# Token tiles normalized on GpSimd, an unmasked pair kept selected behind causal ones, and the gate moved behind the transpose

## The chip, the cores and the metric

The kernel runs on one core of one Trainium2 chip. The metric is the device time of one execution in microseconds, from start to finish, with inputs and outputs in the chip's main memory. Five engines work side by side and each takes its own instructions strictly in order: TensorE (PE, matrix products into the accumulator memory PSUM), VectorE (DVE), ScalarE (ACT), GpSimd (POOL) and SyncE (SP, which here only issues DMA transfers). They wait for one another by semaphores. PSUM has eight banks of 128 x 512 float32.

## The reference

Four residual layers in the order A, B, A, B act on 2048 tokens of width 512 with 32 heads of width 16. Each starts with a layer norm without weights.

```python
def _A_ref(x, wq, wk, wv, wo, beta):      # "infini-attention", 4 segments of 512 tokens
    ...
    for s in range(N):
        logits = einsum('bhqd,bhkd->bhqk', qs, ks) * scale + causal_mask
        a_dot = softmax(logits) @ vs
        a_mem = phi(qs) @ M / (phi(qs) @ z + 1e-6)
        o = g * a_mem + (1.0 - g) * a_dot          # g = sigmoid(beta), one number per head
        M = M + phi(ks)^T @ vs ;  z = z + sum(phi(ks))
    return concat(o) @ wo

def _B_ref(x, wqkv, wo):                   # plain attention, every query against all 2048 keys
    q, k, v = split(x @ wqkv)
    return softmax(q @ k^T * Dh**-0.5) @ v @ wo

x = x + _A_ref(layernorm(x), ...) ; x = x + _B_ref(layernorm(x), ...)    # twice
```

The exponentials dominate: with a head width of 16, a product of queries and keys gives far more elements to exponentiate than it costs to compute.

## The kernel before

The program is written by a Python planner (class `Builder`), which appends instructions to one list per engine. It keeps an estimated end time for every engine and uses these estimates, credits and limits (the class constants) to decide what to append next. The order of each engine's list is therefore fixed when the program is built, and it depends on every constant and every estimated cost, so that a small edit moves instructions all over the program.

**Attention units.** The work of attention is cut into banks, each 128 keys by 512 queries of one head. Eight heads of one 128-row chunk (c = 0 to 3) are treated as two groups of four heads (e = 0, 1). For each group the queries are first masked to its heads (`qm`, line 1159 in `select`): on DVE in a causal group, or while a causal group is selected, or when it is late, otherwise on POOL. A causal group (kind A) has 12 banks for e = 0 and 8 for e = 1, an unmasked group (kind B) has 64, or 16 or 32 in the first round over the keys. Selected groups stand in the list `sel`, and `take_banks` takes three banks at a time from its front. One such unit is: three sets of key-query products on PE into three PSUM banks (six banks alternate), one exponential of 128 x 1536 on ACT (`unit`, line 1244) into `pT`, in a causal unit one or two masks on POOL that zero the part above the diagonal (`affine_select`, line 1259), and two units later the products of `pT` with the values on PE (`pv`). These accumulate in bank 6, the only accumulator. When a group is done, `finish` computes on DVE the reciprocal of the row sums (line 1312), for kind A multiplies it by the gate 1 - g (line 1318), and writes the scaled result `ob` (line 1324). Bank 6 is free for the next group after that.

**Exponentials on DVE.** `dx_pick` may take a bank out of an unmasked group and give it to DVE. Its product goes to bank 7, DVE copies and scales it (`dx_first`, line 910) and runs a chain of five operations on two banks at a time (`dx_chain`, lines 936 to 945). The result `dxo` is used by `pv_taken`. Only selected groups of kind B can give banks, so that nothing can be given while only causal groups are selected.

**Background.** Layer norms, projections, the memory M and the output projections are generators (`task_A`, `task_mem`, `task_B`, `task_out`), of which pieces are put between units (`background`, `bg_one`). A layer norm ends with `normalize` (line 538, DVE), one operation for 128 tokens, whose result `xn` is transposed by a DMA on SP's queue. `ob` is transposed by a DMA into `oT` as well (`run_deferred`). For layers of kind A, `task_out` adds the transposed memory part to `oT` (line 765) and then projects. Projections run on PE in bursts of matmuls of 512 columns into bank 7, evacuated by DVE or ACT (`evac`).

The flag `wide` is set once the first layer A is finished, and lets the DVE chain use more buffers. From layer 1 on, the eight groups of one causal segment of layer 2 (27 units) come between unmasked groups of layer 1. These four stretches are called causal windows below.

Of the kernel before, what the change touches and what calls it, by code (L numbers as in the profile page):

```python
# [3 lines left out]
dt = mybir.dt  # L4
# [252 lines left out]
class Builder:  # L257
    NPU = 4
    WARM, WARM2 = 84, 20
    LAG_A = 2  # L260
    NDX = 4
    FIT, MARGIN = 2, 450
    PART = 3
    FILL_DVE = 300
    EARLY = 400
    FILL = 0.58
    BUSY_COLS = 1024
    DVE_FIN, DX_FIN = 600, 2500
    EVAC_ACT = 0
    DX_BANK, DX_LATE, BG_BANK, DVE_LATE, DVE_LATE_LOW = 500, 3000, 200, 1500, 3500  # L270
    CR_A, CR_B, CR_W, CR_LOW, CARRY, CARRY_W, REST, NEAR, SLACK = 1150, 1500, 1700, 2600, 0, 0, 36, 30, 300
    ALT3, ALT5, GAP, AHEAD, PE_B, PE_A, PE_LOW, LOW, PAIRS, TAKEN, PAIRS2 = 2, 4, 3, 250, 3, 2, 5, 24, 30, 5, 1
# [11 lines left out]
    def alloc(self):  # L284
# [23 lines left out]
        self.qm = sb("qm", [P, 4, 512], bf)  # L308
# [10 lines left out]
        self.gout = sb("gout", [P, H], f32)  # L319
        self.M = sb("M", [P, NCH, 8, 17], f32)  # L320
# [32 lines left out]
        self.b_qm = n1("qm", 4)  # L353
# [7 lines left out]
        self.b_bet, self.b_g, self.b_gout = B("bet"), B("g"), B("gout")  # L361
        self.b_M, self.b_Mn, self.b_Mz = n1("M", 2), B("Mn"), B("Mz")
# [135 lines left out]


# [33 lines left out]
    def normalize(self, s, k, i):  # L533
        t = 4 * s + i
        n = self.ring("xn", 2)
        xn = self.xn[:, n, :]
        mean, rstd = self.lnst[:, k, i, 6:7], self.lnw[:, k, 1, i:i + 1]
        self.op("dve", lambda e: e.tensor_scalar(xn, self.x[:, t, :], mean, rstd, op0=ALU.subtract, op1=ALU.mult),
                reads=[self.b_x[t], self.b_lnst[k][i], self.b_lnw[k]], writes=[self.b_xn[n]], ns=410)
        return n, xn, self.b_xn[n]  # L540
# [213 lines left out]
    def task_out(self, L, s):  # L754
        isA = L % 2 == 0
        wo, bwo = (self.woA, self.b_woA) if isA else (self.woB, self.b_woB)
        for ti in range(4):
# [3 lines left out]
            if isA and s > 0 and ti == 0:  # L761
                for c in range(NCH):
                    yield [("dma", ("oT", L, s, c)), ("dma", ("amemT", L, s, c))], 0, 450
                    o, m = self.oT[:, 0, c, :], self.phq[:, c, :]
                    self.op("dve", (lambda o, m: lambda e: e.tensor_tensor(o, o, m, ALU.add))(o, m),
                            reads=[self.b_phq[c], self.b_oT[0][c]], writes=[self.b_oT[0][c]], ns=420)
# [71 lines left out]
    def dx_pick(self, items):  # L838
# [8 lines left out]
        for n, g in enumerate(self.sel):  # L847
            rest += len(g.banks) - g.pos
            if g.kind != "B" or g.total < 64 and self.near < 150 or g.shut or g.taken >= g.total // (self.TAKEN if self.wide else 6) or rest < (self.REST if self.wide else 30):
# [63 lines left out]

    def dx_close(self):
# [3 lines left out]
    def task_dx(self, k):  # L918
        while True:
# [3 lines left out]
            yield from self.dx_chain(k, b, ents, self.dx_free.pop(0))  # L923

    def dx_chain(self, k, b, ents, slot):
# [6 lines left out]
        out = self.dx_space("out", slot)  # L932
        z, ob = self.dx_space("z", k)[:, 0:w], out.bitcast(dt.int16)[:, 0:w]
        bt, bo, bz = self.b_dxt[b], [self.b_dxo[slot]], [self.b_dxz[k]]
# [6 lines left out]
        self.op("dve", lambda e: e.tensor_scalar(z, z, EXP_B, EXP_A, op0=ALU.mult, op1=ALU.add), reads=bz, writes=bz, ns=ns[1])  # L941
        yield [], 0, c[1]
        self.op("dve", lambda e: e.tensor_tensor(z, z, z, ALU.mult), reads=bz, writes=bz, ns=ns[0])  # L943
        yield [], 0, c[2]
# [46 lines left out]
    def met(self, need):  # L991
# [4 lines left out]
        def ok(n):  # L996
# [6 lines left out]
            if n == "pair":  # L1003
                return len(self.dx_pairs) > 0 and len(self.dx_free) > 0
# [128 lines left out]
    def select(self, late):  # L1133
        tail = self.sel[-2:]
        if len(self.sel) > 2 and self.seqA and self.seqA[0][0].L and all(g.kind == "B" and not g.pos for g in tail) and self.met(self.group_needs(self.seqA[0][0])):
# [5 lines left out]
        while len(self.qm_free) > 1 and (len(self.sel) <= 1 or len(self.sel) == 2 and all(g.kind == "B" and g.total < 64 for g in self.sel)):  # L1141
            pair = None
            for seq in (self.seqA, self.seqB):
                if seq and self.met(self.group_needs(seq[0][0])):
# [356 lines left out]
```

## Time and profile before

| what | value |
|---|---|
| runs | 2001.56, 2004.07, 2004.95 us; median 2004.07 |
| the profiled execution's own time | 2004.62 us |
| its span (first to last instruction) | 2002.9 us |
| ACT busy | 1942.2 us, 97% |
| PE busy | 1721.0 us, 86% |
| DVE busy | 1631.9 us, 81% |
| POOL busy | 270.5 us, 14% |
| granted TensorE clock | 0.988 of full speed |

The profile lists busy time by engine, then groups of instructions (line, engine, operation, tile) with their number, the mean duration of one and the idle time of the engine ahead of them. Two views cut the same execution by time: windows give the busy time of each engine in a stretch, and the timeline gives single instructions, with the idle time of their engine ahead of them and the engine whose instruction ended it. Durations of neighbouring instructions on one engine overlap, so the pitch from start to start is what one costs.

### The profile page before, as it was taken

What the parts mean: (1) busy time and instruction counts of PE and PEld (TensorE: products, weight loads), DVE (VectorE), ACT (ScalarE), POOL (GpSimd) and SP (SyncE); (2) the same over time, 40 slices, a digit from 0 to 9 for tenths busy, and PEclk for the clock granted to TensorE, in tenths of its full rate; (3) what the DMA queues carried; (4) which work ended last, traced back from release to release, by engine and by line L of the source; (5) the groups of instructions that cost most, each with busy time, mean ns of one, the idle gap of its engine ahead of it and who ended that gap; (6) DMA issues with size and microseconds to landing.
All of it is one profiled execution on the core that took longest, in us unless ns stands there. A gap on an engine that the chain in (4) does not pass through costs nothing.

```text
span 2002.9 us, 61442 instructions
## 1 busy us (share of the span) xinstructions
PE 1721.0 (86%) x27135; PEld 890.5 (44%) x27135; DVE 1631.9 (81%) x2979; ACT 1942.2 (97%) x1456; POOL 270.5 (14%) x450
## 2 busy tenths in 40 slices
PE   7888888888878888888888888888888888888888
PEld 4444444444444444444444444444444444444443
DVE  5665555599779895899948996469999999999997
ACT  7899999999999999999999999999999999999998
POOL 3422223110220003100031004101000000000000
PEclk9999999999999999999999999999999999999999
DMA  5111111000100000000011001100000000000000
GB/s 154 33 28 18 31 28 25 4 10 15 18 10 15 5 15 20 18 15 5 15 20 18 5 17 24 20 4 7 15 5 5 5 15 5 5 5 15 5 7 12
DMA packets 100939, 34.76 MB, mean 17 GB/s; under 512 B 93504, under 2 KB 100160, under 8 KB 100672
## 3 DMA queue, kind: packets, MB, share of 16 engines
q1 hardware_dynamic: 100672, 30.83, 8.0%
q8 instruction: 212, 3.47, 0.8%
q14 instruction: 55, 0.45, 0.1%
HBM read 6.30 MB, written 2.10 MB: 4 GB/s over the span
## 4 chain that ended last, share of the span: by engine, by line
ACT 58%; issue 19%; PE 9%; DVE 6%; DMA 1%; POOL 1%; SPq 0%; ACTq 0%; DVEq 0%
ACT pT L1244 57%; PE ps L393 9%; POOL pT L1259 1%; DVE ob L1324 1%; DMA phq<-amem 1%; DVE dxt L910 1%; DVE dxo L945 1%; ACT amem L602 0%; DVE rd L1312 0%; DVE rd L1318 0%; DVE qm L1159 0%; DVE dxz L936 0%; DVE amem L691 0%; DVE KA L910 0%; DVE dxz L939 0%
## 5 line engine op out<-in xcount | busy, mean ns | idle before, releaser
L1244 ACT ACTIVATE pT<-ps 128x1536 bf16<-128x1536 f32 x1413 | 1912.4, 1712 | 43.1 <-PE ps L393 36.0
L393 PE MATMUL ps<-qm,KB 32*128 32x512 bf16 x4096 | 508.8, 386 | 192.9 <-ACT pT L1244 167.0
L393 PE MATMUL ps<-VB,pT 128*128 128x51 bf16 (+1 forms) x14396 | 578.6, 186 | 14.4 <-DVE ob L1324 6.5
L393 PEld LDWEIGHTS ps<-VB,pT 128*128 128x128 bf16 x14396 | 459.6, 96 | 294.5 <-issue 223.5
L393 PEld LDWEIGHTS ps<-qm,KB 32*128 32x128 bf16 x4096 | 130.9, 91 | 525.6 <-ACT pT L1244 487.9
L393 PE MATMUL ps<-wB,zero 128*128 128x512 bf16 x1121 | 357.9, 381 | 0.0
L1259 POOL TENSOR_SCALAR_AFFINE_SELECT pT<-pT 128x768 bf16<-128x768 bf16 (+4 forms) x320 | 176.6, 567 | 510.4 <-ACT pT L1244 509.1
L1159 POOL TENSOR_SCALAR qm<-QB,par 128x512 bf16<-128x512 bf16 x86 | 86.0, 1003 | 1117.2 <-PE ps L393 1097.3
L910 DVE TENSOR_SCALAR dxt<-ps 128x512 uint32<-128x512 f32 x249 | 170.9, 687 | 16.4 <-PE ps L393 14.5
L393 PE MATMUL ps<-VA,pT 128*128 128x51 bf16 (+1 forms) x2560 | 110.5, 190 | 34.6 <-DVE ob L1324 22.8
L393 PEld LDWEIGHTS ps<-VA,pT 128*128 128x128 bf16 x2560 | 85.0, 98 | 77.2 <-POOL pT L1259 37.0
L393 PE MATMUL ps<-qm,KA 32*128 32x128 bf16 (+2 forms) x1536 | 88.7, 260 | 21.8 <-ACT pT L1244 15.1
L393 PE MATMUL ps<-VB,dxo 128*128 128x51 bf16 (+1 forms) x1596 | 104.7, 185 | 0.3 <-DVE dxo L945 0.2
L910 DVE TENSOR_SCALAR KA<-ps 128x512 uint32<-128x512 f32 x125 | 85.7, 686 | 4.6 <-PE ps L393 3.5
L910 DVE TENSOR_SCALAR QA<-ps 128x512 uint32<-128x512 f32 x123 | 84.4, 686 | 5.5 <-PE ps L393 4.9
L939 DVE TENSOR_TENSOR dxz<-dxz 128x1024 f16<-128x1024 f16 (+1 forms) x129 | 86.9, 673 | 0.7
L943 DVE TENSOR_TENSOR dxz<-dxz 128x1024 f16<-128x1024 f16 (+1 forms) x129 | 86.5, 670 | 0.5
L939 DVE TENSOR_TENSOR VA<-VA 128x1024 f16<-128x1024 f16 (+1 forms) x129 | 86.4, 670 | 0.6
L943 DVE TENSOR_TENSOR VA<-VA 128x1024 f16<-128x1024 f16 (+1 forms) x129 | 85.4, 662 | 0.6
L393 PEld LDWEIGHTS ps<-qm,KA 32*128 32x128 bf16 x1536 | 39.1, 93 | 92.6 <-ACT pT L1244 42.3
L393 PEld LDWEIGHTS ps<-wB,zero 128*128 128x128 bf16 x1121 | 78.4, 96 | 0.0
L393 PE MATMUL ps<-xT,wA 128*128 128x512 bf16 x256 | 69.2, 388 | 1.3 <-DVE amem L691 0.4
(124 smaller groups left out, 1601.2 us busy)
## 6 DMA issues: line engine op xcount, KB each, us to landing
out_dram<-x SPq DMA_DIRECT2D x8, 256.0 KB, 2.1
x<-in_A_x_dram SPq DMA_DIRECT2D x3, 512.0 KB, 8.7
wB<-in_B_wqkv_dram SPq DMA_DIRECT2D x1, 1536.0 KB, 12.7
oT<-ob SPq DMA_TRANSPOSE x63, 2.4
xT<-xn SPq DMA_TRANSPOSE x60, 2.5
x<-in_A_x_dram SPq DMA_DIRECT2D x4, 128.0 KB, 2.2
wA<-in_A_wk_dram SPq DMA_DIRECT2D x1, 512.0 KB, 4.3
wA<-in_A_wq_dram SPq DMA_DIRECT2D x1, 512.0 KB, 5.3
```

The costliest lines, as they stand in the source:

```text
L393: self.sc.add("pe", lambda e: e.matmul(out, lhsT, rhs, start=start, stop=stop, skip_group_check=True), reads=reads, banks=[(bank, "w", all ...
L910: self.op("dve", lambda e: e.tensor_scalar(d, o, SCALE * LOG2E * 65536, 126.0 * 65536, op0=ALU.mult, op1=ALU.add), writes=self.dx_writes(" ...
L939: self.op("dve", lambda e: e.tensor_tensor(z, z, z, ALU.mult), reads=bz, writes=bz, ns=ns[0])
L943: self.op("dve", lambda e: e.tensor_tensor(z, z, z, ALU.mult), reads=bz, writes=bz, ns=ns[0])
L945: self.op("dve", lambda e: e.scalar_tensor_tensor(ob, hi, 128.0, z, op0=ALU.mult, op1=ALU.add), reads=bt + bz, writes=self.dx_writes("out" ...
L1159: self.op(eng, (lambda m, q, col: lambda e: e.tensor_scalar(m, q, col, 0.0, op0=ALU.mult, op1=ALU.add))(m, q, col), reads=[bq, self.b_par] ...
L1244: self.sc.add("act", (lambda dst, src: lambda e: e.activation(dst, src, ACT.Exp, scale=SCALE))(dst, src), writes=self.b_pT[slot * 3 + i:sl ...
L1259: self.op("pool", (lambda blk, pat: lambda e: e.affine_select(blk, blk, pattern=pat, compare_op=ALU.is_ge, fill=0.0, base=0, channel_multi ...
L1324: self.op("dve", lambda e: e.tensor_tensor(ob, src[:, :, 0:16], rb, ALU.mult), reads=[br] + bsrc, writes=[self.b_ob[oi][g.e]], bank=bk, al ...
```

## The change

- `normalize` runs on POOL when no causal group is selected and POOL's estimated end lies before that of DVE or PE; otherwise on DVE as before.
- In `select`, once `wide` is set, an unmasked pair may be selected behind causal pairs, and later causal pairs are put ahead of it. The masked queries get six buffers in place of four. As an unmasked group then stands in `sel` while causal units run, `dx_pick` may take banks from it.
- The gate 1 - g leaves `finish`. A new table `gfm` holds it per row of the transposed outputs, and `task_out` multiplies `oT` by it: with `tensor_scalar` in the first segment, and in the others in one operation that also adds the memory part.
- The chain on DVE takes its output buffer only at its last step, with three buffers in place of four; `run_deferred` may leave a transpose for later; at most one taken bank is used per call of `pv_taken`.
- Many constants change: four matmuls of a projection in one piece (PART), other credits (CR_A, CR_B, PE_A, PE_B, CARRY_W), other limits on how late DVE may be.

```diff
 class Builder:
     NPU = 4
+    XN_POOL = 1
+    POOL_T = 0
+    LOOK, PV_TAKEN = 1, 1
+    NQM = 6
+    NEARW = 150
...
-    NDX = 4
+    NDX = 3
-    PART = 3
+    PART = 4
-    EARLY = 400
+    EARLY = 200
-    DVE_FIN, DX_FIN = 600, 2500
+    DVE_FIN, DX_FIN = 600, 9000
-    DX_BANK, DX_LATE, BG_BANK, DVE_LATE, DVE_LATE_LOW = 500, 3000, 200, 1500, 3500
-    CR_A, CR_B, CR_W, CR_LOW, CARRY, CARRY_W, REST, NEAR, SLACK = 1150, 1500, 1700, 2600, 0, 0, 36, 30, 300
-    ALT3, ALT5, GAP, AHEAD, PE_B, PE_A, PE_LOW, LOW, PAIRS, TAKEN, PAIRS2 = 2, 4, 3, 250, 3, 2, 5, 24, 30, 5, 1
+    DX_BANK, DX_LATE, BG_BANK, DVE_LATE, DVE_LATE_LOW = 500, 3000, 200, 1200, 9000000000.0
+    CR_A, CR_B, CR_W, CR_LOW, CARRY, CARRY_W, REST, NEAR, SLACK = 1450, 1750, 1700, 2600, 0, 400, 36, 30, 300
+    ALT3, ALT5, GAP, AHEAD, PE_B, PE_A, PE_LOW, LOW, PAIRS, TAKEN, PAIRS2 = 2, 4, 2, 250, 4, 3, 5, 24, 30, 5, 0
...
+        t, gv = self.gfm[:, NCH:].rearrange("p (c h) -> p c h", h=8), self.gout[:, :].rearrange("p (c h) -> p c h", h=8)
+        hm = bcast(self.hmask[:, 0:1], [[0, NCH], [1, 8]])
+        self.op("dve", lambda e: e.tensor_tensor(t, gv, hm, ALU.mult), reads=[self.b_gout, self.b_hm], writes=[self.b_gfm], ns=190)
+        self.op("dve", lambda e: e.tensor_reduce(self.gfm[:, 0:NCH], t, axis=mybir.AxisListType.X, op=ALU.add),
+                reads=[self.b_gfm], writes=[self.b_gfm], ns=190)
...
-        self.op("dve", lambda e: e.tensor_scalar(xn, self.x[:, t, :], mean, rstd, op0=ALU.subtract, op1=ALU.mult),
-                reads=[self.b_x[t], self.b_lnst[k][i], self.b_lnw[k]], writes=[self.b_xn[n]], ns=410)
+        pool = self.XN_POOL and not self.masks() and self.sc.t["pool"] < max(self.sc.t["dve"], self.sc.t["pe"])
+        self.op("pool" if pool else "dve", lambda e: e.tensor_scalar(xn, self.x[:, t, :], mean, rstd, op0=ALU.subtract, op1=ALU.mult),
+                reads=[self.b_x[t], self.b_lnst[k][i], self.b_lnw[k]], writes=[self.b_xn[n]], ns=900 if pool else 410)
...
-            if isA and s > 0 and ti == 0:
+            if isA and ti == 0:
                 for c in range(NCH):
-                    yield [("dma", ("oT", L, s, c)), ("dma", ("amemT", L, s, c))], 0, 450
-                    self.op("dve", (lambda o, m: lambda e: e.tensor_tensor(o, o, m, ALU.add))(o, m),
+                    o, m, gc = self.oT[:, 0, c, :], self.phq[:, c, :], self.gfm[:, c:c + 1]
+                    if s == 0:
+                        yield [("dma", ("oT", L, s, c))], 0, 360
+                        self.op("dve", (lambda o, gc: lambda e: e.tensor_scalar(o, o, gc, 0.0, op0=ALU.mult, op1=ALU.add))(o, gc),
...
+                        continue
+                    yield [("dma", ("oT", L, s, c)), ("dma", ("amemT", L, s, c))], 0, 700
+                    self.op("dve", (lambda o, m, gc: lambda e: e.scalar_tensor_tensor(o, o, gc, m, op0=ALU.mult, op1=ALU.add))(o, m, gc),
...
+    def masks(self):
+        return any(g.kind == "A" for g in self.sel)
...
     def select(self, late):
-        while len(self.qm_free) > 1 and (len(self.sel) <= 1 or len(self.sel) == 2 and all(g.kind == "B" and g.total < 64 for g in self.sel)):
-            for seq in (self.seqA, self.seqB):
-                if seq and self.met(self.group_needs(seq[0][0])):
-                    pair = seq.pop(0)
-                    break
+        while len(self.qm_free) > 1:
+            look = self.LOOK and self.wide
+            at = next((i for i, g in enumerate(self.sel) if g.kind == "B" and g.e == 0 and not g.pos), len(self.sel)) if look else len(self.sel)
+            few = at <= 1 or not look and at == 2 and all(g.kind == "B" and g.total < 64 for g in self.sel)
...
+            elif self.seqB and at == len(self.sel) and (few or short or look and self.seqB[0][0].total == 64 and all(g.kind == "A" for g in self.sel)) and self.met(self.group_needs(self.seqB[0][0])):
+                pair = self.seqB.pop(0)
...
-                self.sel.append(g)
+                self.sel.insert(at + i, g)
...
     def finish(self, g):
-        if g.kind == "A":
-            h = 8 * g.c + g.e
-            om = bcast(self.gout[:, h:h + 1], [[0, 4], [2, 4]])
-            r4 = rd.rearrange("p (t r) -> p t r", r=4)
-            self.op("dve", lambda e: e.tensor_tensor(r4, r4, om, ALU.mult), reads=[br, self.b_gout], writes=[br], ns=160)
...
     def run_deferred(self, now):
+                if not now and ("op",) + own not in self.flags:
+                    return
...
     def pv_taken(self, g, now, used=()):
-            if r in used:
-                continue
+            if not now and n == self.PV_TAKEN:
+                break
```

## The prediction, made before the changed kernel ran

> **What bounds the kernel now.** I read the engine totals and the groups first, then ACT's waits, then the windows, and last the timeline around single stalls.
>
> ```profile
> PE 1721.0 (86%) x27135; PEld 890.5 (44%) x27135; DVE 1631.9 (81%) x2979; ACT 1942.2 (97%) x1456; POOL 270.5 (14%) x450
> L1244 ACT ACTIVATE pT<-ps 128x1536 bf16<-128x1536 f32 x1413 | 1912.4, 1712 | 43.1 <-PE ps L393 36.0
> ...
> 1439.27 556.25 ACT L1244 ACTIVATE pT<-ps 128x1536 bf16<-128x1536 f32 x414 [0.16 <-PE ps L393]
> ```
>
> ACT is the bound: 1413 exponentials fill 1912.4 us. The last line shows 414 in a row without a gap, so one costs 556.25/414 = 1.344 us. Of the span of 2002.9 us ACT idles 60.7. By stretch:
>
> ```profile
> 0.00:400.00 400.00, 338.74 (x5013) 182.07 (x5013) 227.16 (x547) 363.78 (x280) 111.17 (x211) 0.98 0.20 40
> ...
> 527.00:569.00 42.00, 33.05 (x605) 18.66 (x601) 23.00 (x58) 40.30 (x31) 22.62 (x41) 1.00 0.22 27
> 772.00:816.00 44.00, 36.32 (x593) 19.70 (x591) 24.65 (x55) 41.24 (x32) 22.46 (x41) 0.92 0.14 29
> 1022.00:1065.00 43.00, 34.24 (x597) 19.29 (x593) 25.71 (x58) 40.95 (x32) 23.11 (x41) 0.96 0.22 36
> ...
> 1450.00:1950.00 500.00, 427.88 (x7059) 215.33 (x7058) 492.61 (x780) 500.00 (x374) 20.02 (x19) 1.00 0.03 7
> ```
>
> (Columns: length, then busy time of PE, weight loads, DVE, ACT, POOL, then clock and DMA.) Layer 0 loses 36.2 us of ACT, some 11 of them in the start-up. Three causal windows lose 1.7, 2.8 and 2.1, and there DVE works only 23 to 26 us while POOL masks for 22 to 23. In the unmasked stretches DVE is full (492.61 of 500) and ACT has no gap. The last 53 us lose 6. Two stalls show how ACT loses time:
>
> ```profile
> 88.16 0.18 DVE L1318 TENSOR_TENSOR rd<-rd,gout 128x16 f32<-128x16 f32 x1
> 88.37 0.42 DVE L1324 TENSOR_TENSOR ob<-ps,rd 128x256 bf16<-128x256 f32 x1
> ...
> 88.85 1.40 PE L393 MATMUL ps<-VA,pT 128*128 128x51 bf16 x28 [1.31 <-DVE ob L1324]
> 89.41 1.45 ACT L1244 ACTIVATE pT<-ps 128x1536 bf16<-128x1536 f32 x1 [2.10 <-PE ps L393]
> ```
>
> The gate multiplication stands between a group's reciprocal and the write that frees bank 6; PE waits for it, and ACT for PE. The second is at the end of a causal window:
>
> ```profile
> 567.42 0.88 POOL L1259 TENSOR_SCALAR_AFFINE_SELECT pT<-pT 128x768 bf16<-128x768 bf16 x1 [0.57 <-PE ps L393]
> 567.49 1.36 DVE L936 TENSOR_SCALAR dxz<-dxt 128x1024 f16<-128x1024 uint16 x1
> 568.29 2.21 POOL L1159 TENSOR_SCALAR qm<-QB,par 128x512 bf16<-128x512 bf16 x2
> 568.88 1.06 DVE L939 TENSOR_TENSOR dxz<-dxz 128x1024 f16<-128x1024 f16 x1
> 569.98 0.81 DVE L941 TENSOR_SCALAR dxz<-dxz 128x1024 f16<-128x1024 f16 x1
> ...
> 573.01 1.45 ACT L1244 ACTIVATE pT<-ps 128x1536 bf16<-128x1536 f32 x1 [1.42 <-PE ps L393]
> ```
>
> Chain steps beside POOL take 1.36, 1.06 and 0.81 us, where the same lines alone take 0.69, 0.69 and 0.42. They push `ob` back, and ACT stands 1.42 and then 0.92 us.
>
> **The change, part by part.** The built order of the changed program, which holds no times, gives the counts.
>
> *Banks moved from ACT to DVE.* `dx_first` occurs 512 times, not 497, so 15 banks leave ACT: 1407 full exponentials, one of 1024 and one of 512 columns. Six fewer at 1.344 are -8.1. The two short ones cost at least their share of columns, 0.9 + 0.45 = 1.35, and at most the nearest rows of their widths, 1.08 (the 1024-wide exponential of line 602) and 0.60 (a 512-wide copy): +1.5. ACT evacuates one more projection, +0.6. Sum **-6.0 us** on the engine that sets the end. These are not spread evenly: causal windows of layer 2 go from 3 banks to 39, the unmasked units of layer 1 from 213 to 191.
>
> *DVE's own work.* A bank costs 0.60 for the first step and half of a chain of 0.60 + 0.60 + 0.34 + 0.60 + 1.13 (pitches of lines 936 to 945), 2.24 in all: 15 are +34. 37 of 62 normalizations leave at a pitch of 0.33: -12. The 64 gate products leave at 0.21: -13. The 24 additions to `oT` become `scalar_tensor_tensor` (a 512-wide one takes 0.69, the addition 0.41 alone) and 8 multiplications of 0.35 are new: +9. Net some +18 on 1632, of no price by itself, since the causal windows leave DVE 17 to 19 us idle each.
>
> *Gate.* Each causal group frees bank 6 by 0.21 earlier. In layer 0 PE waited 18 times for `ob`, which makes 18 x 0.21 = 3.8 us at most; counting PE's work in its first 54 units by pitches of the timeline (0.215 us for 512 columns, 0.031 for a value product, some 0.4 for the products of a unit) gives 1.39 us per unit, above ACT's 1.344, so nearly all of it passes on: -3. In layer 2 PE has slack: -0.5 (0 to -4). Total **-3.5**. The price is a longer step ahead of the output projection, covered by groups that are already selected; the cover ends where a segment runs out (next).
>
> *Layer 0's order.* PE has the same work (364 projection matmuls become 368). A new gap appears behind the last causal unit of segment 1: one unit of a single bank, then four value projections of 4 matmuls (1.04 us each) before the next unit can start; ACT has 2.3 us of other work meanwhile, so 2 to 3 us stay. In return the bursts that caused the gaps of 1.76, 2.10 and 1.70 us between 81 and 93 us go. The constants reorder the rest; PE's count above one unit's time rises by some 6 us over the layer on paper, and the idle that can be won is 25. I take **-1** (+6 to -8).
>
> *Causal windows.* Projection matmuls in the first three fall from 93 to 20, and with them the bursts behind the 6.5 us of idle: -3 (0 to -6.5). In their place DVE runs the chain there. For the second window I count 34.4 us of DVE work (20.4 in operations like those of 567 us: chain, `qm`, phi; 14 in operations that read PSUM) in 27 units, 36.3 us of exponentials plus three of 1.08 for phi, 39.5. POOL's masks take 22.4 us. How long the 37 operations of the first kind are held up is not shown for a full window. The low end is `qm` on DVE inside today's windows:
>
> ```profile
> L1159 DVE TENSOR_SCALAR qm<-QA,par x64: 340/348/1210, 13.3 to 1240.1; 128x512 bf16<-128x512 bf16 x64
> ```
>
> Its group's mean is 0.441, so 0.09 each; 34.4 + 37 x 0.09 = 37.7 still fits in 39.5. The high end is the trio at 567 us, 0.48 each: 52.2, which after 1.2 us of lateness that the planner allows is 11.5 too long per window. `qm` is nearest, being in the same windows among the same masks, but finishes want DVE at once, so I put 1 us per window: **+3** (0 to +35).
>
> *More bursts between windows.* The 73 matmuls moved out make 18 bursts more in unmasked units. Today's 79 bursts there left two gaps, of 1.1 and 1.6 us: 18/79 x 2.7 = 0.6. DVE is fuller there now, so I take **+1.5** (0 to +4).
>
> *Normalizing on POOL.* No such row exists; POOL's `qm` of the same size takes 0.69 at least and 1.00 in the mean, DVE's `xn` 0.42. On POOL it stands behind `qm` that may wait 25.8 us for their buffer, which the planner's test on POOL's estimated end avoids. On SP 37 transposes wait for POOL, and with them the `oT` transposes queued behind, up to 0.7 us each. Both feed projections whose groups are not yet due: 0. If that cover is gone: 37 x 0.6 = +22.
>
> Sum: -6.0 - 3.5 - 1 - 3 + 3 + 1.5 = -9.0. The profiled execution took 2004.62 us (1.7 outside the span), 0.55 above the median of the three runs; **1995.6 us**.
>
> **The rivals.**
>
> *The shared port makes DVE the bound of the causal windows (slower).* Place: the three windows with 12 or 13 taken banks. It decides from a hold-up of 0.25 us per operation: without my +3 and -3, 9.0 of gain stand against 3 x (34.4 + 37 d - 40.7). At d = 0.34, the middle from there to the trio's price, this is +19: 2004.6 - 9.0 + 18.9 = **2014.5** (2008 to 2030). For it: masks fill 22.4 of 39.5 us, the 567 us case, and DVE's plan is 87% full. Against it: the `qm` row, and that 14 us of DVE's work can pass beside masks. The Trainium skill, "SBUF — State Buffer", section "Who interferes with whom", says that GpSimd and such DVE operations hold one port pair exclusively, the second fully waiting; the trio agrees. By that rule 20.4 + 22.4 = 42.8 us must go through the pair, 3.3 more than 39.5 per window, and the sum would come to some 2005.
>
> *Nothing is left.* Late `xn`, the new gap of layer 0 at +6 and its other reordering eat the 9: **2003** (2000 to 2008). For it: 36 of ACT's idle lie in a layer that no count of banks touches. Against: layer 0's order of groups is nearly the same, and PE's work too.
>
> *Layer 0 and the windows empty out.* Upper ends for gate, layer 0 and bursts: -6 - 4 - 8 - 6.5 + 1.5 = -23: **1982**. That every bound holds together is unlikely.
>
> That the change does nothing is excluded by the order: 37 `xn` on POOL, 39 banks in the causal windows.
>
> **How the numbers follow.** Forecast 0.58 (own range 1987 to 2000), slower by the port 0.22, nothing left 0.13, large gain 0.07. About 0.2%, 4 us, is what this kernel's runs can tell from no change. Faster 0.65, same 0.13, slower 0.22. The range from 1985 to 2014 leaves out half of the port's case and most of the large gain, under 2 in 10.
>
> **What would show it.** Right: 1407 exponentials of 1536 columns, ACT idle near 53 us; DVE above 33 us in each of the first three causal windows and ACT idle there no more than 3; `ob` waits in layer 0 shorter. Wrong: lines of the chain with means well above 0.69 in these windows, masks well above 0.56, and PE waiting there for `ob` or `qm`; or an `xn` on POOL above 1 us with PE waiting for the projection's input.

## The result, and the profile after

The changed kernel took **2026.75 us** in the median of three runs (2026.4 to 2028.62) against 2002.9 us before: a ratio of 1.012, 95% interval 1.0101 to 1.0139. One more execution, the one profiled first, had a much lower TensorE clock towards its end and took 2146.05 us; with it the median is 2027.7. The kernel is slower by some 24 us; forecast was a gain of 9. The profile below is of another execution of the same kernel, with a span of 2031.6 us and a time of its own of 2033.32 us, 6.6 us above the median.

The engine totals and three groups of its page (busy time, mean ns of one, then idle time ahead and its main cause):

```profile
PE 1741.2 (86%) x27132; PEld 906.0 (45%) x27132; DVE 1662.0 (82%) x2933; ACT 1938.4 (95%) x1453; POOL 371.9 (18%) x483
...
L1287 ACT ACTIVATE pT<-ps 128x1536 bf16<-128x1536 f32 x1409 | 1907.5, 1655 | 72.6 <-PE ps L400 66.5
...
L1302 POOL TENSOR_SCALAR_AFFINE_SELECT pT<-pT 128x256 bf16<-128x256 bf16 (+4 forms) x320 | 194.3, 624 | 402.8 <-ACT pT L1287 400.5
...
L552 POOL TENSOR_SCALAR xn<-x,lnst,lnw 128x512 bf16<-128x512 bf16 x37 | 93.9, 2542 | 416.4 <-DVE lnw L543 395.4
```

ACT works 3.8 us less, where the banks moved to DVE were to bring 6.0, but stands idle for 93.2 us (2031.6 - 1938.4) in place of 60.7. POOL gained 101 us of work, of which 37 normalizations are 93.9: one takes 2.54 us in the mean. The waits of the whole execution (engine, what it waited for, us in total, times, longest):

```profile
ACT pT L1287 <- PE ps L400: 66.5, 81, 4.6
...
PE ps L400 <- DMA xT<-xn: 16.3, 7, 3.8
```

ACT waited 36.0 us for PE before, 2.3 at most; now there are waits of 4.6. For transposed `xn` PE waited 0.8 us before, in two waits; now it waits 16.3, in seven. One of them in the timeline (start, duration, engine, instruction, idle time ahead and its cause):

```profile
484.49 6.37 POOL L552 TENSOR_SCALAR xn<-x,lnst,lnw 128x512 bf16<-128x512 bf16 x2 [2.69 <-DMA xT<-xn]
...
487.40 4.67 SPq L434 DMA_TRANSPOSE xT<-xn  x2
...
493.54 1.86 PE L400 MATMUL ps<-xT,wA 128*128 128x512 bf16 x4 [3.30 <-DMA xT<-xn]
...
496.74 6.82 ACT L1287 ACTIVATE pT<-ps 128x1536 bf16<-128x1536 f32 x5 [4.25 <-PE ps L400]
...
501.33 1.04 PE L400 MATMUL ps<-xT,wA 128*128 128x512 bf16 x4
```

Two normalizations take 6.37 us on POOL, their transposes end behind them, and PE, which takes its list in order, stands 3.30 us in front of a projection, with the next unit's products behind it. ACT then loses 4.25 us. The four matmuls behind the stall take 1.86 us, and four of the same shape at 501 us 1.04. The granted clock tells why (columns as in the prediction):

```profile
484.00:492.00 8.00, 5.31 (x84) 2.40 (x79) 7.37 (x12) 8.00 (x7) 6.37 (x2) 0.97 0.25 51
492.00:500.00 8.00, 6.46 (x84) 3.60 (x84) 4.39 (x7) 3.75 (x4) 0.00 (x0) 0.60 0.16 33
```

It falls from 0.97 in the first 8 us to 0.60 in the next; read in steps of 0.2 us, it stands at 0.50 from 491.6 to 498.2 us. So this wait of PE cost more than its own length. The Trainium skill, "TensorE: Matmul & The Clock Gate", section "Part 1: The HAM clock gate (the "warmup" mystery)", states that TensorE falls back to half its clock after an idle window of about 3.4 us. The half agrees with this trace (0.50, and 1.86 against 1.04 us), the length doesn't: PE's last matmul ended at 490.24, and the clock fell some 1.3 us later; behind the stalls of 1.93 and 1.88 us that end at 996.4 and 1221.6 us it fell to 0.50 as well.

The second place is the causal windows. ACT's idle time in four stretches, each from 4 us before the window's first mask to 8 us behind its last, and outside of them, summed from the windows view (us):

| kernel | layer 0, 0 to 400 us | 400 to 1420 us | of it the four causal windows |
|---|---|---|---|
| before | 36.2 | 18.5 | 14.2 |
| after | 37.1 | 48.0 | 25.6 |

So 11.4 us of the loss arose in the causal windows, and some 18 outside of them, where the prediction's steps had +1.5 for bursts and 0 for the normalization.

### The profile page after: what moved, and what is told of

The parts are those of the page before. It is cut to its first block, busy times and chain, and to the rows that moved or that the text cites. A ratio compares the mean times of both kernels' runs of the same rounds, so it can differ in the third digit from the quotient of the medians.

```text
span 2144.3 us, 61426 instructions
## 1 busy us (share of the span) xinstructions
PE 1861.3 (87%) x27132; PEld 944.3 (44%) x27132; DVE 1663.1 (78%) x2933; ACT 1941.2 (91%) x1453; POOL 371.7 (17%) x483
## 4 chain that ended last, share of the span: by engine, by line
ACT 33%; issue 17%; DVE 15%; PE 15%; POOL 3%; DMA 2%; ACTq 0%; DVEq 0%; POOLq 0%; SPq 0%
ACT pT L1287 33%; PE ps L400 15%; POOL xn L552 2%; DVE dxo L971 2%; DVE dxt L930 2%; DMA xT<-xn 1%; DVE KA L930 1%; DVE QA L930 1%; DVE dxz L967 1%; DVE dxz L962 1%; DVE dxz L959 1%; DVE VA L962 1%; DVE VA L971 1%; DVE VA L959 1%; DVE VA L967 1%
## 5 line engine op out<-in xcount | busy, mean ns | idle before, releaser
L400 PE MATMUL ps<-qm,KB 32*128 32x512 bf16 x4096 | 560.6, 411 | 167.3 <-ACT pT L1287 139.1
L400 PEld LDWEIGHTS ps<-VB,pT 128*128 128x128 bf16 x14336 | 489.1, 98 | 330.3 <-issue 251.1
L400 PE MATMUL ps<-VB,pT 128*128 128x51 bf16 (+1 forms) x14336 | 611.9, 191 | 19.3 <-DVE ob L1363 11.5
L400 PE MATMUL ps<-wB,zero 128*128 128x512 bf16 x1118 | 401.5, 425 | 0.0
L1302 POOL TENSOR_SCALAR_AFFINE_SELECT pT<-pT 128x256 bf16<-128x256 bf16 (+4 forms) x320 | 194.7, 625 | 398.6 <-ACT pT L1287 397.7
L1202 POOL TENSOR_SCALAR qm<-QB,par 128x512 bf16<-128x512 bf16 x82 | 76.8, 943 | 689.7 <-PE ps L400 615.9
L552 POOL TENSOR_SCALAR xn<-x,lnst,lnw 128x512 bf16<-128x512 bf16 x37 | 93.9, 2541 | 415.0 <-DVE lnw L543 393.9
L400 PE MATMUL ps<-VB,dxo 128*128 128x34 bf16 (+1 forms) x1528 | 108.1, 193 | 0.3 <-DVE dxo L971 0.2
L1355 DVE RECIPROCAL rd<-ps 128x16 f32<-128x16 f32 x112 | 28.0, 250 | 90.7 <-PE ps L400 89.7
L962 DVE TENSOR_TENSOR VA<-VA 128x1024 f16<-128x1024 f16 (+1 forms) x132 | 90.6, 687 | 0.7
L967 DVE TENSOR_TENSOR VA<-VA 128x1024 f16<-128x1024 f16 (+1 forms) x132 | 90.6, 686 | 0.4
```

The costliest lines, as they stand in the source:

```text
L400: self.sc.add("pe", lambda e: e.matmul(out, lhsT, rhs, start=start, stop=stop, skip_group_check=True), reads=reads, banks=[(bank, "w", all ...
L552: self.op("pool" if pool else "dve", lambda e: e.tensor_scalar(xn, self.x[:, t, :], mean, rstd, op0=ALU.subtract, op1=ALU.mult), reads=[se ...
L1202: self.op(eng, (lambda m, q, col: lambda e: e.tensor_scalar(m, q, col, 0.0, op0=ALU.mult, op1=ALU.add))(m, q, col), reads=[bq, self.b_par] ...
L1302: self.op("pool", (lambda blk, pat: lambda e: e.affine_select(blk, blk, pattern=pat, compare_op=ALU.is_ge, fill=0.0, base=0, channel_multi ...
L1355: self.op("dve", lambda e: e.reciprocal(rd, src[:, :, 16]), reads=bsrc, writes=[br], bank=bk, alloc=al, ns=253)
```

## The experiments

Three theories stood at the start. Theory 1: GpSimd's slow normalization makes PE wait. Theory 2: the pair kept selected crowds the causal windows, DVE's chain beside POOL's masks. Theory 3: the new constants gave a worse order of the work.

**e1, the changed kernel again.** It gave the profile above.

> The changed kernel once more, for a profile at the usual clock. All theories: 2026 to 2029 us. The first profile of it showed 2.54 us for a normalization on GpSimd in place of the 0.69 to 1.00 that the prediction took, and five long gaps of ScalarE (3.12, 1.23, 4.63, 2.20 and 2.27 us) behind such normalizations, 13.5 us together; between 400 and 1350 us ScalarE idled 47.7 us where it idled 18.4 before. If these belong to the kernel and not to that execution, they are here again: normalization 2.1 to 2.6 us, gaps of 12 to 15 us behind it, and 6 to 10 us of gaps in each of the first three causal windows.

2033.32 us, one execution, above the 2026 to 2029 that were expected. The slow normalizations and the five gaps are there again.

**e2, the 37 normalizations back on DVE at the same places.** The planner keeps its estimates, so the lists of PE, ACT and SP are those of the changed kernel.

```diff
-        self.op("pool" if pool else "dve", lambda e: e.tensor_scalar(xn, ...), ..., ns=900 if pool else 410)
+        self.sc.add("dve", lambda e: e.tensor_scalar(xn, ...), ..., ns=900 if pool else 410, est="pool" if pool else None)
```

> The 37 normalizations run on VectorE at the same places, and every other instruction of every engine keeps its place. Theory 1 (the slow normalization on GpSimd makes transposes late and TensorE waits for them): the five gaps of 13.5 us close, 2012 to 2016 us. Theory 2 (the shared port in the causal windows is the cause): these windows hold no normalization, so at most 3 us change, 2024 to 2028 us. Theory 3 (the new order of the instructions costs the time, whatever engine normalizes): 2026 to 2030 us, or more, as VectorE gets 12 us of work back.

2017.76 us, ratio 1.0077 (1.0058 to 1.0096). It lies between the theories' numbers: theory 1 carries time, but not all of it. The windows are as idle as after (table below).

**e3, no normalization on POOL, planned anew; e4, no unmasked pair behind causal ones, planned anew.**

```diff
-    XN_POOL = 1
+    XN_POOL = 0          # e3
-    LOOK, PV_TAKEN = 1, 1
+    LOOK, PV_TAKEN = 0, 1   # e4
```

> The switch for normalizing on GpSimd is off and the planner orders anew, so VectorE gives up some banks (503 taken, not 512, 35 of them in causal units): 3 banks of 0.45 us each per unit make ScalarE 4.0 us longer. Theory 1: 13.5 gained, 4.0 lost, 2016 to 2020 us. Theory 2: 2028 to 2033 us. Theory 3: cannot be told, as the order is another.

> No unmasked pair behind causal ones: 493 banks taken, 7 of them in causal units; normalization stays on GpSimd. ScalarE gets 19 banks more, 8.5 us. Theory 1: the gaps behind normalizations stay, and the time grows by the 8.5 us less what the causal windows give back (0 to 6): 2030 to 2036 us. Theory 2: the causal windows give back 17 us: 2017 to 2021 us. If both hold, 2019 to 2030 us.

e3 took 2005.87 us, ratio 1.0023 (1.0012 to 1.0034); e4 2011.81 us, ratio 1.0044 (1.0027 to 1.0061). Both lie below every range that the theories gave, e4 also below the 2019 to 2030 for both theories together, so both parts seem to matter. But a new plan moves everything, and e2 and e3 differ by 12 us with the normalization on DVE in both, so these runs don't give sizes. The next ones keep the order.

**e5, the masks of layer 2 cut to one column; e6, the three middle steps of DVE's chain cut to 8 columns while a causal group is in front.** Both stand on e2, with its order. In e6 the first step of the chain and the last keep their width: the program leaves the last step whole, though the expectation counts it among the shortened ones. The trace shows it: in the first three windows 15 of the 18 second steps (line 964) have 8 columns, while all 15 last steps (line 973) have 1024.

```diff
+                if items[i][0].L == 2:
+                    dims = [[1, 1]]              # e5
...
+        n = lambda: 8 if self.sel and self.sel[0].kind == "A" else w      # e6: width m of the three middle steps
...
-        self.op("dve", lambda e: e.tensor_tensor(z, z, z, ALU.mult), reads=bz, writes=bz, ns=ns[0])
+        self.op("dve", (lambda m: lambda e: e.tensor_tensor(z[:, 0:m], z[:, 0:m], z[:, 0:m], ALU.mult))(n()), reads=bz, writes=bz, ns=ns[0])
```

> The kernel of e2 (normalizations back on DVE at the same places, 2017.8 us), and every causal mask of layer 2 shortened to one column. It leaves out the causal mask of layer 2; the order of every engine's list is that of e2. Theory 'port': DVE's chain in the causal windows is held up by POOL's masks. Then chain steps there return to 0.6 to 0.7 us, ACT's idle time in the four windows falls from some 24 us to 8 or less, and the time is 1998 to 2006. Theory 'load': DVE is simply too full there, the masks are not to blame; then the time stays at 2014 to 2020. If the gaps come from PE (its own work and a lower clock), it stays as well.

> The kernel of e2, and the three middle steps and the last step of DVE's chain and its half-way multiplication shortened to 8 columns wherever a causal group is in front (the first step of each bank, which reads PSUM, stays whole). It leaves out part of the exponentials taken in the causal windows; the order of every list is that of e2. Both theories 'port' and 'load' expect that ACT's idle time in the windows falls from some 24 us to 8 or less and the time to 1998 to 2006. If PE's own work causes the gaps there (more products and weights per unit, a lower clock), the time stays at 2013 to 2020.

e5 took 1992.72 us, ratio 0.9935 (0.991 to 0.996), which is 25 us less than e2; e6 took 2007.17 us, 1.0014 (1.0 to 1.0028), 11 less. So the masks carry the loss in the windows, and the chain is a part of it; the theory "load" alone, which left e5 at 2014 to 2020, falls. Two expectations were missed: e5 lies below the 1998 to 2006 of the theory "port", and e6, for which both theories expected 1998 to 2006 and 8 us of idle time or less in the windows, keeps 17.6 us there (table below). How much of these belongs to the two steps that stayed whole, no run shows. DVE's groups in the third window of e2 and then of e5 (count, busy us, mean ns, then idle time):

```profile
L963 DVE TENSOR_TENSOR VA<-VA 128x1024 f16<-128x1024 f16 x3 | 3.2, 1066 | 0.1
L1203 DVE TENSOR_SCALAR qm<-QA,par 128x512 bf16<-128x512 bf16 x6 | 3.1, 550 | 0.0
L963 DVE TENSOR_TENSOR dxz<-dxz 128x1024 f16<-128x1024 f16 x3 | 2.9, 970 | 0.1
...
L965 DVE TENSOR_SCALAR VA<-VA 128x1024 f16<-128x1024 f16 x3 | 2.1, 686 | 0.1
```

```profile
L963 DVE TENSOR_TENSOR VA<-VA 128x1024 f16<-128x1024 f16 x3 | 2.1, 690 | 0.1
...
L963 DVE TENSOR_TENSOR dxz<-dxz 128x1024 f16<-128x1024 f16 x3 | 2.1, 689 | 0.1
...
L1203 DVE TENSOR_SCALAR qm<-QA,par 128x512 bf16<-128x512 bf16 x6 | 1.8, 346 | 0.0
...
L965 DVE TENSOR_SCALAR VA<-VA 128x1024 f16<-128x1024 f16 x3 | 1.3, 427 | 0.1
```

In the same order, line 963 takes 0.69 us without full masks beside it, and 0.97 to 1.07 with them; line 965 goes from 0.43 to 0.69 and `qm` from 0.35 to 0.55. Over the first three windows the four chain lines 960 to 968 of e2 stand 0.05 to 0.21 us above e5, the last step 0.15, and `qm` 0.16: in the mean about 0.15 each. POOL pays as well: between the kernel before and e2 the masks of 768 columns go from 0.87 to 1.09 us, those of 256 from 0.46 to 0.57, those of 128 from 0.31 to 0.60. So the delay is mutual. The Trainium skill, "SBUF — State Buffer", section "Who interferes with whom", states that VectorE and GpSimd share one port pair as an exclusive lock, and that whoever issues first holds it for the whole instruction while the other waits. That both engines are delayed agrees; whether a single operation waits out the other's whole length, the means of 0.05 to 0.29 us can't show.

**e14, the same cut of the masks in the kernel before.** e5 takes away the masks' own cost as well, which this run separates; nothing else changes, the order included.

> The kernel before, the same order on every engine, with the causal masks of layer 2 shortened to one column (it leaves out the causal mask of layer 2). Theory 'port': masks cost where DVE's chain runs beside them, of which there is little here: 1996 to 2001 beside 2003, at most 7 us gained, against 25 in e5. Rival 'masks cost by themselves, by PE's wait for them': 1978 to 1988, the same 15 to 25 us as in e5.

1995.2 us, ratio 0.9963 (0.995 to 0.9976): 7 to 8 us are the masks by themselves, against 25 in e5. So some 17 us of e5's gain hang on what is new in e2's windows. That this is the chain beside the masks is shown for a part of it, by the 11 us of e6; for the rest it is argued from the longer durations.

**e7 and e15, the normalization in eight forms.** By the tile's number in its segment, four forms each.

```diff
-        ... tensor_scalar(xn, self.x[:, t, :], mean, rstd, op0=ALU.subtract, op1=ALU.mult)
+        forms = [(mean, rstd, ALU.subtract, ALU.mult), (rstd, mean, ALU.mult, ALU.add), (mean, 1.0, ALU.subtract, ALU.mult), (rstd, 0.0, ALU.mult, ALU.add)]   # e7
+        forms = [(rstd, mean, ALU.mult, ALU.subtract), (mean, rstd, ALU.add, ALU.mult), (mean, 1.0, ALU.add, ALU.mult), (rstd, 0.0, ALU.mult, ALU.subtract)]   # e15
+        s1, s2, o0, o1 = forms[i]
```

> The changed kernel, with the normalization written in four forms by the tile's number in its segment: 0 as it is (subtract one operand per row, multiply by another), 1 multiply by an operand per row and add another, 2 subtract an operand per row and multiply by 1.0, 3 multiply by an operand per row and add 0.0. Forms 1 to 3 leave out or change the normalization of three tiles in four; the order is that of the changed kernel. If the second operand per row makes the GpSimd operation slow: forms 0 and 1 take 2.0 to 2.6 us, forms 2 and 3 take 0.7 to 1.2. If it is the subtraction: 0 and 2 are slow. If it is the place (the neighbours on the engine or on DVE), all four take 2.0 us or more. The time: 2020 to 2032 in the first two cases, 2026 to 2034 in the last.

> The changed kernel with four other forms of the normalization by the tile's number: 0 multiply by an operand per row, subtract another; 1 add an operand per row, multiply by another; 2 add an operand per row, multiply by 1.0; 3 multiply by an operand per row, subtract 0.0 (all leave out or change the normalization). If the subtraction is what is slow: forms 0 and 3 take 2.0 us or more, 1 and 2 take 0.7 to 1.0. If it is a first operation other than a multiplication: 1 and 2 are slow, 0 and 3 take 0.7 to 1.0. Time 2010 to 2030.

The tile view of `xn` (count, then min/median/max in ns), of e7 and then of e15:

```profile
L554 POOL TENSOR_SCALAR xn<-x,lnst,lnw x12: 2069/2341/3150, 106.1 to 1290.4; 128x512 bf16<-128x512 bf16 x12
...
L554 POOL TENSOR_SCALAR xn<-x,lnst x11: 1995/2010/3721, 111.9 to 1295.3; 128x512 bf16<-128x512 bf16 x11
L554 POOL TENSOR_SCALAR xn<-x,lnw x10: 690/696/1715, 113.9 to 1297.3; 128x512 bf16<-128x512 bf16 x10
...
L554 POOL TENSOR_SCALAR xn<-x,lnw,lnst x4: 766/922/1636, 196.1 to 1197.9; 128x512 bf16<-128x512 bf16 x4
```

```profile
L554 POOL TENSOR_SCALAR xn<-x,lnw,lnst x12: 2069/2288/3146, 106.0 to 1290.1; 128x512 bf16<-128x512 bf16 x12
...
L554 POOL TENSOR_SCALAR xn<-x,lnst x11: 690/710/2196, 111.9 to 1295.0; 128x512 bf16<-128x512 bf16 x11
L554 POOL TENSOR_SCALAR xn<-x,lnw x10: 1994/2207/3292, 112.6 to 1296.3; 128x512 bf16<-128x512 bf16 x10
...
L554 POOL TENSOR_SCALAR xn<-x,lnst,lnw x4: 765/920/1636, 195.5 to 1197.5; 128x512 bf16<-128x512 bf16 x4
```

(`lnst` holds the mean, `lnw` one over sigma, and the inputs stand in the order of use.) In all four forms with a subtraction, first or second, with one operand or two, the shortest takes 1.99 to 2.07 us. In all four of multiplication and addition it takes 0.69 (one operand per row) or 0.77 (two). On DVE nothing of this shows: in the median one operand takes 0.34 to 0.35 and two take 0.41, with a subtraction or without. So it is the subtraction on GpSimd, and neither the operands nor the place. The times, one execution each, were 2013.27 us, below the 2020 to 2032 expected, and 2012.84 us, within 2010 to 2030.

**e9 and e13, the normalization without subtraction.** The whole normalization is kept: x times 1/sigma plus -mean/sigma, which one small DVE operation makes for four tiles. The order is that of the changed kernel; e13 repeats e9 for a profile of its waits.

```diff
+        o = self.op("dve", lambda e: e.scalar_tensor_tensor(tt, st[:, k, :, 6], -1.0, y, op0=ALU.mult, op1=ALU.mult), ...)
...
-        ... e.tensor_scalar(xn, self.x[:, t, :], mean, rstd, op0=ALU.subtract, op1=ALU.mult)
+        ... e.tensor_scalar(xn, self.x[:, t, :], rstd, nmr, op0=ALU.mult, op1=ALU.add)
```

> The changed kernel, the same order on every engine, with the normalization written as x times 1/sigma plus a second operand, -mean/sigma, that one DVE operation of 128 x 4 makes for four tiles. If the subtraction alone makes GpSimd slow: 0.75 to 1.0 us on POOL in place of 2.07 and more, ACT's long gaps behind the transposes (about 15 us in the changed kernel) fall below 4, and the time is 2011 to 2018. If a normalization on POOL costs by its place in the queue, whatever its duration: 2022 to 2030.

> The kernel of e9 again, for its waits. 2008 to 2016 us; the normalization on POOL 0.76 us at least and about 0.9 in the median; ACT's gaps behind the transposes under 4 us together in place of about 15; idle time in the four causal windows still 20 to 26 us.

e9 took 2012.77 us, ratio 1.0046 (1.0027 to 1.0064), e13 2009.27. Against the changed kernel's 1.012 that is 0.0074, or 15 us, for the subtraction alone. The tile view of `xn` and the waits of e13:

```profile
L556 POOL TENSOR_SCALAR xn<-x,lnw x37: 762/990/2326, 106.7 to 1289.3; 128x512 bf16<-128x512 bf16 x37
...
  PE ps L400: 0.8, 1
```

```profile
ACT pT L1291 <- PE ps L400: 44.6, 76, 2.5
```

PE waits for a transposed `xn` once, 0.8 us, in place of 16.3, and ACT's longest wait for PE falls from 4.6 to 2.5.

**e10, e9 without the pair behind causal groups; e11, neither of the two parts.** Both planned anew.

```diff
-    LOOK, PV_TAKEN = 1, 1
+    LOOK, PV_TAKEN = 0, 1   # e10, on e9; e11 on the changed kernel, with XN_POOL = 0 too
```

> e9 with no unmasked pair selected behind causal ones (planned anew, so the order differs). If the slow subtraction and the causal windows are the two causes and add up: idle time of ACT in the windows about 8 us, no long gap behind the transposes, 1997 to 2004. If something third is in the new constants and the order: 2007 to 2013, as without the pair alone.

> The changed kernel with normalizations on DVE and no unmasked pair behind causal ones (planned anew): what is left is the gate's move, the chain's buffers and the constants. If these are as good as the prediction's other terms (gate, fewer bursts in the windows): 1996 to 2003. If the constants' order is a cause of its own: 2006 to 2014.

e10 took 2003.91 us, ratio 1.0005 (0.9991 to 1.0019); e11 2001.67 us, 0.9996 (0.9981 to 1.0011). Each is the kernel before within what can be told. The two causes account for the loss: 15 us for the subtraction, measured in the same order, and 8 (1.0046 to 1.0005) for the pair, measured with a new order, so that this size is less certain. Theory 3 has nothing left: the new constants alone are no worse. But they are no better either, where the gate, layer 0 and fewer bursts in the windows were to bring 7.5 us. ACT's idle time shows the reason:

| kernel | layer 0 | 400 to 1420 us | of it the windows | exponential units, short ones too |
|---|---|---|---|---|
| before | 36.2 | 18.5 | 14.2 | 1413 |
| after | 37.1 | 48.0 | 25.6 | 1409 |
| e2, normalization on DVE | 26.4 | 41.1 | 26.3 | 1409 |
| e5, and masks cut | 28.6 | 19.4 | 7.0 | 1409 |
| e6, and three chain steps cut | 27.7 | 32.7 | 17.6 | 1409 |
| e13, no subtraction | 29.8 | 31.4 | 21.6 | 1409 |
| e10, and no pair | 29.9 | 18.6 | 8.8 | 1415 |
| e11, neither | 29.2 | 14.9 | 9.6 | 1419 |
| e14, before with masks cut | 35.7 | 11.3 | 6.3 | 1413 |

e11 idles 7.0 us less in layer 0 and 3.6 less behind it, and has six exponentials more, two of them short, since fewer banks are taken without the pair: ACT works 6.1 us more (1948.3 against 1942.2). The pair turns this round: ACT works 5.5 us less in e13 than in e10 (1938.0 against 1943.5), and idles 12.8 us more in the windows.

The third window (1013 to 1070 us of e13, 1019 to 1072 of before) is the worst: ACT idles 8.5 us there in e13 and 2.1 before, while the other three together differ by 1.0 only. There one sees what PE waits for, of e13 and then of before:

```profile
PE ps L400 <- DVE ob L1367: 7.4, 8, 1.7
PE ps L400 <- POOL pT L1306: 3.9, 8, 0.9
```

```profile
PE ps L393 <- DVE ob L1324: 3.4, 5, 1.0
PE ps L393 <- POOL pT L1259: 1.8, 4, 0.8
```

And one case of it in e13's timeline:

```profile
1034.19 1.53 DVE L975 SCALAR_TENSOR_TENSOR dxo<-dxt,VA 128x1024 int16<-128x1024 uint16 x1
...
1035.65 0.68 DVE L934 TENSOR_SCALAR KA<-ps 128x512 uint32<-128x512 f32 x1
...
1036.25 0.24 DVE L1359 RECIPROCAL rd<-ps 128x16 f32<-128x16 f32 x1
1036.52 0.42 DVE L1367 TENSOR_TENSOR ob<-ps,rd 128x256 bf16<-128x256 f32 x1
...
1037.01 1.03 PE L400 MATMUL ps<-VA,pT 128*128 128x51 bf16 x24 [0.93 <-DVE ob L1367]
```

The last step of a chain, stretched to 1.53 us, and the next bank's first step stand ahead of the group's finish. `ob` is late, bank 6 is not free, and PE waits.

The clock adds to it. In the changed kernel's four windows the granted clock, read in steps of 0.2 us, stands at half for 52.7 us in place of 22.4 before, and 17.0 of the 25.6 us of idle time fall into these stretches, in place of 5.7 of 14.2. So, in sum, all of the 11.4 us more lie where PE runs at half its clock. One such stretch, of 10.2 us, begins 1.6 us after a wait of PE of 1.67 us for `ob` (1049.84 us), and ACT idles 2.3 us in it. The waits come first in the trace, but no run separates their own cost from that of the clock: in e6's third window PE's waits for `ob` fall from 7.3 to 2.4 us (e2 and e6), while the clock there is 0.74 in the mean and ACT still idles 8.2 us in place of 9.8.

**e8, e12 and e16, the gate alone.** e8 makes only the gate's move in the kernel before, planned anew. e12 takes the multiplication out of the kernel before and puts nothing in its place, in the same order. e16 moves the gate in segments 1 to 3, in the same order on PE, ACT, POOL and SP.

```diff
-            self.op("dve", lambda e: e.tensor_tensor(r4, r4, om, ALU.mult), reads=[br, self.b_gout], writes=[br], ns=160)   # e8, e12; e16 unless segment 0
...
-                    self.op("dve", (lambda o, m: lambda e: e.tensor_tensor(o, o, m, ALU.add))(o, m), ...)
+                    self.op("dve", (lambda o, m, gc: lambda e: e.scalar_tensor_tensor(o, o, gc, m, op0=ALU.mult, op1=ALU.add))(o, m, gc), ...)   # e8, e16
```

> The kernel before with nothing but the gate's move: no multiplication behind the reciprocal, transposed outputs multiplied by the table of gates, all constants as before. The prediction's term says -3.5 us: 1997 to 2000 beside a kernel before of 2001.5, with shorter waits of PE for the scaled result in layer 0. Rival: DVE has slack there or a new order eats it: within 1.5 us of the kernel before. A gain of more than 6 us would mean that the term was too small.

> The kernel before, the same order on every engine, without the multiplication by the gate and with nothing in its place (it leaves out the factor 1 - g). This is the upper bound of what the gate's move can bring. The prediction's term says -3 in layer 0 and -0.5 in layer 2: 1997.5 to 2001 beside a kernel before of 2002 to 2004, ratio 0.997 to 0.999. Rival: PE is not the bound of layer 0's units, and the time does not change (within 1 us).

> The kernel before, the same order on PE, ACT, POOL and SP, with the gate moved to the transposed outputs in segments 1 to 3 of the causal layers (inside the addition that is there already) and left behind the reciprocal in segment 0. Three quarters of what e12 gained (5.8 us): 1997 to 2000.5 beside 2003, ratio 0.9970 to 0.9985. Rival: the longer operation ahead of the output projection eats it, ratio 0.999 to 1.001.

e8 took 2097.09 us, ratio 1.0462 (1.0439 to 1.0486), which nothing had foreseen. Its loss lies in layer 0, where ACT is idle for 123.6 of 400 us (36.2 before):

```profile
165.06 0.60 ACT L420 ACTIVATE KA<-ps 128x512 bf16<-128x512 f32 x1 [4.66 <-PE ps L395]
170.31 0.60 ACT L420 ACTIVATE KA<-ps 128x512 bf16<-128x512 f32 x1 [4.66 <-PE ps L395]
189.79 2.79 ACT L1259 ACTIVATE pT<-ps 128x1536 bf16<-128x1536 f32 x2 [18.88 <-PE ps L395]
```

Projections and the output projection stand one behind the other while no group can be selected, so ACT has nothing to do. I take it that, with the constants of before, one more step ahead of the output projection upsets the planner; no run tests that, and e8 says nothing on the gate's price. e12 does: 1996.48 us, ratio 0.9971 (0.9957 to 0.9986), so 5.8 us (2.8 to 8.6) are the most that the move can bring in this order. e16 took 2003.58 us, ratio 1.0002 (0.9993 to 1.0011): with three quarters of the multiplications gone and the additions turned into the longer operation, nothing was gained. Why the rest of e12's 5.8 us did not come, I can't say: the gain in segment 0 was left out, and the longer operation takes 0.74 us in the median in place of 0.42, 24 times, but no run separates the two.

## Why the prediction was wrong

**The step that failed first is *Normalizing on POOL*, taken as 0.** Its price rested on `qm`, "0.69 at least and 1.00 in the mean", as the nearest row. `qm` and `xn` have the same instruction name and the same size, and `xn` took 2.07 us at least and 2.54 in the mean. The reason is the arithmetic operation: `qm` multiplies, `xn` subtracts. The cover went with it: "groups are not yet due" held for normalizations of 0.99 us in the median (e13), and not for two normalizations of 6.37 us with their transposes behind them, since PE can't pass the projection. The upper bound named there, 37 x 0.6 = +22, used a wrong duration for every tile, where the cost came at a few places: five gaps of 14.9 us in sum (4.25, 1.22, 4.62, 2.48, 2.34). Layer 0 differs by 7.3 us more between the two profiles (37.1 and 29.8), which lie 6.6 us above and 3.5 below the medians of their kernels, so that 14.9 and the measured 15 us agree by chance. That the 15 us lie inside the bound is luck too, and no case carried them: "nothing is left" let late `xn` and layer 0 eat 9 us together and no more. The planner shares the error: its estimate for this operation was 0.9 us.

***Causal windows*, the term of +3, was too small.** Its place and mechanism were right: DVE's chain beside POOL's masks, PE waiting there for `ob`. The idle time there is 12.8 us more with the pair than without (e13, e10), 10.2 of them in the three windows that the term counts. The size was wrong because of the arithmetic that I used. It asked whether DVE's work still fits into a window, with a break-even of 0.25 us for each operation. The measured hold-up is about 0.15, which by that sum (34.4 + 37 x 0.15 = 40.0 against 40.7) costs nothing. But a bank that PE needs is late by a whole chain step well before DVE is full, and the masks get longer as well, which the sum left out, as it did the clock that falls when PE waits. In the third window of e13 DVE works 50.0 of 56.4 us and POOL 32.6. So the rival "the shared port makes DVE the bound" named the right neighbours and the wrong condition: neither engine is full, they are late. The prediction's sign for its first part was right: without the pair the windows' idle time falls from 14.2 to about 9 (in the first three, which it counted, by 1.9 to 2.1), -3 having been forecast.

***Banks moved from ACT to DVE*, -6.0:** ACT's work fell by 3.8 us in the changed kernel and by 4.2 in e13 (1942.2 to 1938.0). The step held in direction, a third less in size. e10 shows that it hangs on the pair: without it there are six exponentials more.

***Gate* and *Layer 0's order*, -4.5 together:** layer 0 idles 6.4 to 7.0 us less in e13 and e11, so the sum of the two was about right; which of the two it is stays open, since e16 gave nothing and e12 5.8. In the changed kernel itself the slow normalization hid all of this (37.1 against 36.2).

***More bursts between windows*, +1.5:** outside the windows, between 400 and 1420 us, e11 idles 5.3 us and before 4.3, which agrees; e10 and e13, with normalizations of about 1 us on POOL, idle 9.8 there. e2, which has the order of e13 and no normalization on POOL, idles 14.8 there, so POOL alone isn't the reason; what part the plan has, no run shows.

What the prediction's last part named as the sign of error came: "an `xn` on POOL above 1 us with PE waiting for the projection's input". The other came as well: in the first three windows of the changed kernel the chain's first two steps take 0.84 and 0.85 us in the mean, and PE waits 18.2 us for `ob`, in place of 9.9.

No run was faster than the kernel before with all of the work done: e11's interval, 0.9981 to 1.0011, includes no change.

## What to carry to other kernels

A duration is a matter of the engine, the shape and the arithmetic operation: before an operation is moved to GpSimd, look for a row there with the same operation, and write a subtraction as a multiplication and an addition. Where DVE and GpSimd work in the same stretch, don't only ask whether DVE's work still fits; ask which result with a deadline stands behind a stretched operation, and look at the granted clock behind PE's waits. And a change that steers a planner is split with its order held fixed: a new plan moved the time by as much as the parts themselves (e2 and e3, 12 us; e8, 93 us).

## What was not expected of the hardware

- On GpSimd a `tensor_scalar` of 128 x 512 bf16 takes 0.69 us with one operand per row and 0.77 with two, but 1.99 to 2.07 with a subtraction in it, in either place; on DVE the forms differ by less than 0.07 us.
- A stall of PE of 3.30 us was followed by matmuls of 0.46 us in place of 0.26 (1.86 and 1.04 for four). The granted clock fell to 0.50 some 1.3 us after PE's last matmul and stayed there for 6.6 us; stalls of 1.9 us were enough as well.
- Beside DVE's chain, the smallest masks on POOL (128 columns) doubled, from 0.31 to 0.60 us, while those of 768 columns grew by a quarter, from 0.87 to 1.09. With the chain's middle steps cut (e6) the smallest took 0.39, and the largest 1.03.
